# First expert's differences all on VectorE, its successor's chunks loaded under the projection, the first tile's splits dealt out later

## The chip, the cores and the metric

One Trainium2 chip, one of its cores. The metric is the time of one execution on the device in microseconds (us), the median of the runs; smaller is better. TensorE does the matmuls and transposes (PE; its weight loads are PEld), VectorE (DVE), ScalarE (ACT) and GpSimd (POOL) work elementwise, SyncE (SP) issues transfers. Each engine takes its instructions in program order, and so does each engine's queue of transfers it issues.

## The reference, cut to what matters

Attention with a mask of hash buckets gives x (1536 tokens of 512), a first layer takes the largest of three products, and a second layer sends each token to one of eight experts:

```
attn_out = _attn_ref(q, k, v, proj)                    # 2 x 8 heads x 768 x 64
x = attn_out.transpose(0, 2, 1, 3).reshape(1536, 512)
h = maximum(maximum(x @ w1, x @ w2), x @ w3)           # 1536 x 768
x = h @ w_out                                          # the projection, 1536 x 512
out = x
for tokens with x @ w_skip > 0:
    e = argmax(x @ w_gate)                             # one of 8 experts
    out += softmax weight of e * (relu(x @ w1[e]) @ w2[e])   # 512 -> 1024 -> 512
```

## The kernel before, in words

All matmuls of the two layers work on splits: a float32 value is cut into a high part of TensorE's fp32r type and the rest, and a product is made of three matmuls (high by high, high by low, low by high). A split is two instructions, a copy on ScalarE that makes the high part and a subtraction that makes the low part.

The stretch around the change has two stages. The first is the projection, the loop over T in `fused_kernel` (lines 264 to 291): twelve tiles of 128 tokens, 18 matmuls each (line 270) into one of four accumulators `po`. After them `gsplit` splits the input of tile T + 2 (ScalarE line 164, VectorE line 165), a step of the routing is issued (T = 0 to 5), ScalarE evacuates `po` into one of three buffers `x2` (line 278; the last tile on VectorE, line 280), and SyncE writes `x2` twice, to `x2d` for later gathers and to the output (lines 281 and 282). Then come one chunk load and, in tiles 2 to 9, two splits of expert 0's weights. The routing's fourth step (T = 3) has GpSimd scatter the tokens' places into a list, twelve indirect transfers (line 481), and load the list back as `LT` (line 488). After tile 8 GpSimd gathers the first 128 rows of expert 0 into `xf[0]` by that list, if they all lie in the first nine tiles (line 513).

The second stage is `moe2`: for each expert a tile of its first 128 tokens, then as many extra tiles as it needs. With these inputs the trace shows one tile for each expert, five extra ones for expert 0 and one for expert 7. A tile transposes its rows and splits them (`turn`, lines 546 and 550, 551), multiplies by w1 in two halves (`mm1`, line 570), takes the relu on ScalarE (line 575), transposes and splits the hidden rows (`hidden`), multiplies by w2 (`mm2`, line 583), weighs and adds (`finish`, line 588) and scatters the rows to the output (line 590). The rows of an expert's first extra tile, `xe`, are gathered by GpSimd (line 513 in `pull`) in the middle of its first tile.

Each expert's weights are eight chunks of 512 KB, chunk i of expert e being number 8 e + i. A chunk lies in a ring slot until it is split, by 16 splits k = 0 to 15 for an expert, two for a chunk (line 375 on ScalarE, line 377 on VectorE, or on GpSimd for k in `POOLK` = 3, 7, 11, 15). The second split of a chunk frees its slot. The ring has five slots under the projection and nine in `moe2`. `load` takes the next chunk if a slot is free and otherwise does nothing; its transfer waits on SyncE until the slot's last split is done. In an expert's first tile the next expert's 16 splits are dealt out at five places by `aside(k)`, k splits with a load behind each. The order of all instructions is the program's; nothing is rearranged.

Of the kernel before, what the change touches and what calls it, by code (L numbers as in the profile page):

```python
# [89 lines left out]
def fused_kernel(ctx, tc, qk, qz, v, vt, proj, cst, pat, w123, wo, woT, wg, e1, e2, out, upto=9, dbg=None):  # L90
# [68 lines left out]
    def gsplit(T):  # L159
        pool, bufs = (tpool, 2) if T % 3 else (gpool, 1)  # L160
        h = pool.tile([P, NF1, P], F32R, tag="gh", name="gh", bufs=bufs)
        l = pool.tile([P, NF1, P], F32R, tag="gl", name="gl", bufs=bufs)
        src = g[:, :, T * P:(T + 1) * P]
        nc.scalar.activation(out=h, in_=src, func=AF.Copy)
        nc.vector.tensor_tensor(out=l, in0=src, in1=h.bitcast(F32), op=ALU.subtract)
        gs[T] = h, l
# [3 lines left out]
    with tc.tile_pool(name="wpb", bufs=1, side=LEFT, reuse_waits="tile") as wpb:  # L170
# [32 lines left out]
        for f in range(NF1):  # L203
# [4 lines left out]
            for j in range(NBLK):  # L208
                b, a = divmod(j * BLK, S)
                pts = []  # L210
                for w in range(3):
                    pt = ps1.tile([P, BLK], F32, tag="m", name="m", bufs=6)
                    pts.append(pt)
                    n = 0
# [31 lines left out]
        for i in range(2):  # L246
            a, e = 512 * i, min(512 * i + 512, S)
# [7 lines left out]
    m2 = Moe2Weights(tc, nc, e1, e2, m2p)  # L255
# [4 lines left out]
    with tc.tile_pool(name="ps2", bufs=1, space=PSUM, reuse_waits="tile") as ps:  # L260
        steps = routing(tc, nc, ps, tpool, rpool, zs, wlg, g, ident, onesb, trib, cc, lst, rt)
        m2.load(3)
        gsplit(1)
        for T in range(NTT):
            po = ps.tile([P, DM], F32, tag="po", name="po", bufs=4)
            h, l = gs.pop(T)
            n = 0
            for f in range(NF1):
                for a, r in ((h, woh), (h, wol), (l, woh)):
                    nc.tensor.matmul(po, lhsT=a[:, f], rhs=r[f], start=(n == 0), stop=(n == 3 * NF1 - 1))  # L270
                    n += 1
            if T + 2 < NTT:
                gsplit(T + 2)
            if steps:
                steps.pop(0)()
            x2 = tpool.tile([P, DM], F32, tag="x2", name="x2", bufs=3)
            if T + 1 < NTT:
                nc.scalar.activation(out=x2, in_=po, func=AF.Copy)
            else:
                nc.vector.tensor_copy(out=x2, in_=po)  # L280
            nc.sync.dma_start(out=x2d[T * P:(T + 1) * P, :], in_=x2)
            nc.sync.dma_start(out=out[T * P:(T + 1) * P, :], in_=x2)
            m2.load(min(1, Moe2Weights.NCH - m2.loaded))
            for k in SPLITS.get(T, ()):
                m2.split(0, k)
            if T == EARLY:
                rt["plan"] = [nc.values_load(rt["plan"][0:1, e:e + 1], engines=ENGINES) for e in range(E2)]
            if T == EARLY - 1:
                early = nc.values_load(rt["early"], engines=[mybir.EngineType.Pool])
                with tc.If(early > 0):  # L290
                    fetch(nc, xf[0], x2d[0:EARLY * P], rt["LT"][:, 0])
# [23 lines left out]
class Moe1Weights:  # L315
# [20 lines left out]
    def split(self, f, w, pool, tag, bufs):  # L336
        self.narrow(f, w, pool, tag, bufs)
        self.halves(f, w)


class Moe2Weights:
# [29 lines left out]
    def split(self, e, k):  # L371
        i, q = divmod(k, 2)
        a = slice(q * 512, q * 512 + 512)
        h, l, r = self.hi[e % 2][i][:, a], self.lo[e % 2][i][:, a], self.raw[e, i][:, a]
        self.nc.scalar.activation(out=h, in_=r, func=AF.Copy)  # L375
        eng = self.nc.gpsimd if k in POOLK else self.nc.vector
        eng.tensor_tensor(out=l, in0=r, in1=h.bitcast(F32), op=ALU.subtract)  # L377
        if q:
            self.free.append(self.raw.pop((e, i)))
# [11 lines left out]
def routing(tc, nc, ps, pool, keep, zs, wlg, g, ident, onesb, trib, cc, lst, rt):  # L391
    def fold():
        t2 = ps.tile([P, NF1, 32], F32, tag="t2", name="t2", bufs=1)
        for f in range(NF1):
            nc.tensor.matmul(t2[:, f], lhsT=zs[:, f * P:(f + 1) * P], rhs=cc[:, 32:64],
                             start=True, stop=True, skip_group_check=True)
        nc.scalar.activation(out=wlg, in_=t2, func=AF.Copy)

    def logits():
        lg = ps.tile([P, BLK], F32, tag="lg", name="lg", bufs=1)  # L400
        for f in range(NF1):
            for j in range(NBLK):
                nc.tensor.matmul(lg[32 * j:32 * j + 32, :], lhsT=wlg[:, f], rhs=g[:, f, j * BLK:(j + 1) * BLK],
                                 start=(f == 0), stop=(f == NF1 - 1), skip_group_check=True)
        rt["lgs"] = pool.tile([P, BLK], F32, name="lgs")
        nc.scalar.activation(out=rt["lgs"], in_=lg, func=AF.Copy)

    return [fold, logits, *route(tc, nc, ps, pool, keep, rt, ident, onesb, trib, cc, lst)]
# [103 lines left out]
def fetch(nc, xg, x2d, m):  # L512
    nc.gpsimd.indirect_dma_start(out=xg, out_offset=None, in_=x2d,  # L513
                                 in_offset=bass.IndirectOffsetOnAxis(ap=m[:, 0:1], axis=0))


def moe2(tc, nc, m2, ident, rt, XF, x2d, out):
# [8 lines left out]
    with tc.tile_pool(name="ps3", bufs=1, space=PSUM, reuse_waits="tile") as ps:  # L526
# [7 lines left out]
        def enlist(e):  # L534
            nc.gpsimd.tensor_copy(out=PL[0][:, 0:CMAX - 1], in_=LT[:, e * CMAX + 1:(e + 1) * CMAX])  # L535
# [24 lines left out]
        def hidden(d, n):  # L560
            d["hT", n] = h, l = [pool.tile([P, 4, P], F32R, tag="t" + x, name="t" + x, bufs=2) for x in "hl"]
            halves(turn(d["r", n]), h, l)

        def mm1(d, n, cr):
            if ("h", n) not in d:
                d["h", n] = ps.tile([P, 512], F32, tag="h", name="h", bufs=3)
            h, l = d["x"]
            for c in cr:
                for i, (a, lo) in enumerate(((h, 0), (h, 1), (l, 0))):
                    nc.tensor.matmul(d["h", n], lhsT=a[:, c], rhs=m2.w1(d["e"], c, n, lo),  # L570
                                     start=(c == 0 and i == 0), stop=(c == NC1 - 1 and i == 2))

        def relu(d, n):
            d["r", n] = pool.tile([P, 512], F32, tag="r", name="r", bufs=2)
            nc.scalar.activation(out=d["r", n], in_=d["h", n], func=AF.Relu)

        def mm2(d, fr):
            if fr[0] == 0:
                d["y"] = ps.tile([P, DM], F32, tag="y", name="y", bufs=2)
            for f in fr:  # L580
                h, l = d["hT", f // 4]
                for i, (a, lo) in enumerate(((h, 0), (h, 1), (l, 0))):
                    nc.tensor.matmul(d["y"], lhsT=a[:, f % 4], rhs=m2.w2(d["e"], f, lo),  # L583
                                     start=(f == 0 and i == 0), stop=(f == NF2 - 1 and i == 2))

        def finish(d):
            ot = d["xg"]
            nc.vector.scalar_tensor_tensor(out=ot, in0=d["y"], scalar=d["m"][:, 2:3].bitcast(F32),
                                           in1=ot, op0=ALU.mult, op1=ALU.add)
            nc.gpsimd.indirect_dma_start(  # L590
                out=out, out_offset=bass.IndirectOffsetOnAxis(ap=d["m"][:, 1:2], axis=0),
                in_=ot, in_offset=None, bounds_check=NT - 1, oob_is_err=False)

        def tile(d, aside=lambda k: None, ahead=lambda: None, then=lambda: None):
            aside(4)
            mm1(d, 0, (0, 1, 2, 3))
            relu(d, 0)
            aside(4)
            mm1(d, 1, (0, 1))
            hidden(d, 0)  # L600
            mm1(d, 1, (2, 3))
            relu(d, 1)
            ahead()
            aside(4)
            mm2(d, (0, 1))
            hidden(d, 1)
            aside(3)
            mm2(d, (2, 3))
            then()
            aside(1)  # L610
            mm2(d, (4, 5, 6, 7))
            finish(d)

# [25 lines left out]
        for e in range(E2):  # L639
            todo = list(range(16)) if e + 1 < E2 else []  # L640

            def aside(k):
                for j in todo[:k]:
                    m2.split(e + 1, j)
                    m2.load(1)
                del todo[:k]

            m2.load(sum(RING) if e == 0 else 0)

            def ahead():  # L650
                enlist(e)
                pull(0)
                hint(e, 0)

            def then():
                prepare(e + 1)
                gather(e + 2)

            tile(tiles[e], aside, ahead, then)
            extras(tiles[e])  # L660
# [415 lines left out]
ENGINES = [mybir.EngineType.PE, mybir.EngineType.Activation, mybir.EngineType.DVE, mybir.EngineType.Pool]  # L1076
EARLY = 9
SPLITS = {T: (2 * T - 4, 2 * T - 3) for T in range(2, 10)}
POOLK = (3, 7, 11, 15)
def lay_out(q, k, v, proj, moe_w1, moe_w2, moe_w3, moe_w_out, moe2_w_skip, moe2_w_gate, moe2_w1, moe2_w2):  # L1080
    tr = [a.transpose(0, 1, 3, 2).reshape(B * NPAIR, 2, D, S) for a in (q, k)]
# [36 lines left out]
```

## Time and profile before

| | us |
|---|---|
| median of 3 runs | 713.81 |
| lowest and highest | 713.08 and 721.5 |
| the profiled execution, whole | 718.32 |
| its span, first to last instruction | 716.5 |
| busy in it: TensorE | 654.8 (91%) |
| VectorE | 421.4 (59%) |
| ScalarE | 336.9 (47%) |
| GpSimd | 317.1 (44%) |
| mean granted TensorE clock | 0.966 |

The profile is one execution; the rows below are from it, with times counted from the start of its span. Its own time lies between the lowest and the highest of the runs. The page cuts the span into 40 slices of 17.9 us; TensorE's busy tenths stand there beside the clock, the transfers and the other engines, and the views by instruction, by wait and by transfer tell what is behind a slice.

### The profile page before, as it was taken

Reading aid. Unit: us, or ns where it says so; the run is one execution under the profiler, and the core shown is the slowest. Engines: PE = TensorE matmul, PEld = TensorE weight load, DVE = VectorE, ACT = ScalarE, POOL = GpSimd, SP = SyncE. Lnnn points to the kernel's source line nnn. Section 1 sums busy time; section 2 is a strip of 40 time slices with the busy share of each in tenths; the row PEclk is TensorE's granted clock in tenths of the full one; section 3 lists DMA queues with packets and bytes.
Section 4 is the critical chain, followed back from the end, with each engine's and each line's share of the span. In section 5 each row is a group of like instructions: output and inputs, shape, how many; then the busy total and the mean of one; then the engine's idle time right before and its main releaser. Section 6 shows DMA issues by size and latency. Waiting matters only on the chain. (4 is left out here: it accounts for less than half of the span.)

```text
span 716.5 us, 9581 instructions
## 1 busy us (share of the span) xinstructions
PE 654.8 (91%) x3361; PEld 479.9 (67%) x3361; DVE 421.4 (59%) x648; ACT 336.9 (47%) x648; POOL 317.1 (44%) x250
## 2 busy tenths in 40 slices
PE   6789999999999988999999999987899988987784
PEld 2544555555555547999999997865688866665563
DVE  4696868878785582656656652723422267777611
ACT  6664666766665651323222312533422256766521
POOL 2494767767677760322221200452512055555630
PEclk9798999999999999999999999999999999999997
DMA  6444314213003003114303133348911047667510
GB/s 250 166 155 138 104 45 155 68 47 108 23 1 114 0 1 148 46 74 147 136 29 130 60 118 110 126 149 302 403 39 44 31 167 271 223 242 259 192 45 12
DMA packets 31472, 87.40 MB, mean 122 GB/s; under 512 B 4066, under 2 KB 4450, under 8 KB 30608
## 3 DMA queue, kind: packets, MB, share of 16 engines
q1 hardware_dynamic: 28144, 78.21, 30.9%
q0 software_dynamic: 3232, 8.07, 3.7%
q8 instruction: 40, 0.66, 0.4%
q14 instruction: 56, 0.46, 0.2%
HBM read 77.35 MB, written 10.18 MB: 122 GB/s over the span
## 5 line engine op out<-in xcount | busy, mean ns | idle before, releaser
L831 POOL TENSOR_TENSOR sum<-sum,Pt 128x768 f32<-128x768 f32 x60 | 116.8, 1950 | 33.6 <-ACT Pt L826 33.5
L826 ACT ACTIVATE Pt<-psb 128x384 f32<-128x384 f32 x192 | 83.8, 488 | 65.7 <-PE psb L824 64.8
L791 DVE TENSOR_REDUCE negm<-psa 128x1 f32<-128x768 f32 x86 | 82.0, 954 | 46.6 <-PE psa L789 46.3
L217 PE MATMUL m<-xh,whi 128*128 128x384 f32 x288 | 98.3, 341 | 3.0 <-DVEq L922 2.9
L377 DVE TENSOR_TENSOR w2l<-ring,w2h 128x512 fp32r<-128x512 f32 x96 | 76.0, 839 | 40.5 <-ACT w2h L375 36.6
L217 PE MATMUL m<-xl,whi 128*128 128x384 f32 x288 | 97.3, 338 | 0.0
L217 PE MATMUL m<-xh,wlo 128*128 128x384 f32 x288 | 97.3, 338 | 0.0
L375 ACT ACTIVATE w2h<-ring 128x512 fp32r<-128x512 f32 x128 | 72.0, 622 | 29.0 <-DMA ring<-in_dram 14.8
L838 PE MATMUL pso<-Pt,V 128*64 128x384 f32 x384 | 83.8, 518 | 0.2 <-DVE negm L791 0.2
L822 PE MATMUL psb<-S 128*128 128x384 f32 x192 | 76.5, 398 | 0.3 <-ACT S L766 0.3
L822 PEld LDWEIGHTS psb<-S 128*128 128x128 f32 x192 | 37.2, 194 | 54.1 <-ACT Pt L826 21.5
L824 PE MATMUL psb<-S 128*128 128x384 f32 x192 | 66.1, 344 | 0.0
L377 POOL TENSOR_TENSOR w2l<-ring,w2h 128x512 fp32r<-128x512 f32 x32 | 43.9, 1382 | 45.5 <-ACT w2h L375 14.3
L217 PEld LDWEIGHTS m<-xh,whi 128*128 128x128 f32 x288 | 54.6, 190 | 6.0 <-DVEq L922 3.5
L583 PE MATMUL y<-w2h,th 128*128 128x512 f32 x112 | 49.1, 439 | 6.5 <-ACT th L550 5.8
L217 PEld LDWEIGHTS m<-xl,whi 128*128 128x128 f32 x288 | 54.7, 190 | 0.0
L217 PEld LDWEIGHTS m<-xh,wlo 128*128 128x128 f32 x288 | 54.5, 189 | 0.0
L583 PE MATMUL y<-w2h,tl 128*128 128x512 f32 x112 | 47.1, 421 | 7.9 <-DVE tl L551 7.9
L334 POOL TENSOR_TENSOR wlo<-wide,whi 128x512 fp32r<-128x512 f32 x18 | 23.4, 1300 | 69.4 <-ACT whi L333 54.2
L551 DVE TENSOR_TENSOR tl<-tp,th 128x512 fp32r<-128x512 f32 x28 | 19.3, 688 | 56.4 <-ACT th L550 51.2
L570 PE MATMUL h<-w2h,xh 128*128 128x512 f32 x112 | 46.2, 413 | 5.5 <-ACTq L619 2.6
L789 PE MATMUL psa<-S 128*128 128x512 f32 (+1 forms) x172 | 47.6, 359 | 0.9 <-ACT S L766 0.8
(185 smaller groups left out, 1219.2 us busy)
## 6 DMA issues: line engine op xcount, KB each, us to landing
ring<-in_dram SPq DMA_DIRECT2D x64, 512.0 KB, 6.2
R<-in_dram SPq DMA_DIRECT2D x32, 384.0 KB, 3.1
wraw<-in_dram SPq DMA_DIRECT2D x6, 1536.0 KB, 6.4
Z<-in_dram SPq DMA_DIRECT2D x16, 384.0 KB, 5.5
V<-in_dram SPq DMA_DIRECT2D x8, 384.0 KB, 3.6
oraw<-in_dram SPq DMA_DIRECT2D x6, 512.0 KB, 3.4
traw<-in_dram SPq DMA_DIRECT2D x6, 512.0 KB, 4.3
x2d<-x SPq DMA_DIRECT2D x12, 256.0 KB, 2.3
```

The lines of the kernel that those rows point to most:

```text
L217: nc.tensor.matmul(pt, lhsT=l[:, w, c], rhs=r[b][c][:, a:a + BLK], start=(n == 0), stop=(n == 3 * NC1 - 1))
L375: self.nc.scalar.activation(out=h, in_=r, func=AF.Copy)
L377: eng.tensor_tensor(out=l, in0=r, in1=h.bitcast(F32), op=ALU.subtract)
L570: nc.tensor.matmul(d["h", n], lhsT=a[:, c], rhs=m2.w1(d["e"], c, n, lo), start=(c == 0 and i == 0), stop=(c == NC1 - 1 and i == 2))
L583: nc.tensor.matmul(d["y"], lhsT=a[:, f % 4], rhs=m2.w2(d["e"], f, lo), start=(f == 0 and i == 0), stop=(f == NF2 - 1 and i == 2))
L789: nc.tensor.matmul(tl[:, a:e], lhsT=S1[:, h, t * P:(t + 1) * P], rhs=S1[:, 2 + h, a:e], start=True, stop=True, skip_group_check=True)
L791: nc.vector.tensor_reduce(out=d["negm"][:, t, h:h + 1], in_=tl[:, 0:S], axis=AX.X, op=ALU.max, negate=True)
L822: nc.tensor.matmul(tl, lhsT=S1[:, 2 + h, k * P:(k + 1) * P], rhs=S1[:, h, cut(j)], start=True, stop=False, skip_group_check=True)
L824: nc.tensor.matmul(tl, lhsT=S2[:, 2 + h, k * P:(k + 1) * P], rhs=S2[:, h, cut(j)], start=False, stop=True, skip_group_check=True)
L826: nc.scalar.activation(out=pt[:, cut(j)], in_=tl, func=AF.Exp, scale=0.125)
L831: eng.tensor_tensor(out=d["sum", h], in0=d["P", h, 0] if k == 1 else d["sum", h], in1=pt, op=ALU.add)
L838: nc.tensor.matmul(d["o"][64 * h:64 * h + 64, i], lhsT=d["V"][:, k, h], rhs=d["P", h, k][:, i * BLK:(i + 1) * BLK], start=(k == 0), stop=( ...
```

## The change

Three edits. Under the projection `m2.load(1)` runs in every tile, so chunks of expert 1 follow those of expert 0 as slots come free. The subtractions of expert 0's splits are all VectorE's; for other experts k = 3, 7, 11 and 15 stay GpSimd's. And `aside` takes the number of the place instead of a count: in expert 0's first tile the counts are 0, 4, 4, 4, 4, in the others 4, 4, 4, 3, 1 as before.

```
-            m2.load(min(1, Moe2Weights.NCH - m2.loaded))
+            m2.load(1)
...
-        eng = self.nc.gpsimd if k in POOLK else self.nc.vector
+        eng = self.nc.gpsimd if e and k in POOLK else self.nc.vector
...
-        def tile(d, aside=lambda k: None, ahead=lambda: None, then=lambda: None):
-            aside(4)
+        def tile(d, aside=lambda n: None, ahead=lambda: None, then=lambda: None):
+            aside(0)
             mm1(d, 0, (0, 1, 2, 3))
             relu(d, 0)
-            aside(4)
+            aside(1)
             mm1(d, 1, (0, 1))
             hidden(d, 0)
             mm1(d, 1, (2, 3))
             relu(d, 1)
             ahead()
-            aside(4)
+            aside(2)
             mm2(d, (0, 1))
             hidden(d, 1)
             aside(3)
             mm2(d, (2, 3))
             then()
-            aside(1)
+            aside(4)
             mm2(d, (4, 5, 6, 7))
             finish(d)
...
-            def aside(k):
+            def aside(n):
+                k = DEAL[e > 0][n]
                 for j in todo[:k]:
                     m2.split(e + 1, j)
                     m2.load(1)
...
+DEAL = (0, 4, 4, 4, 4), (4, 4, 4, 3, 1)
```

## Rows read from the trace of the kernel before

**Rows 1.** Timeline, TensorE: start, us, line, operation, [idle before, what ended it].
```profile
483.80 0.79 PE L270 MATMUL po<-woh,gh 128*128 128x512 f32 x1 [2.85 <-ACT gh L164]
...
490.64 0.63 PE L546 MATMUL tp<-cs,xf 128*128 128x128 f32 x4 [0.92 <-DMA lst<-dt,posi]
491.95 0.50 PE L570 MATMUL h<-w2h,xh 128*128 128x512 f32 x1 [0.69 <-ACT xh L550]
...
503.51 0.50 PE L583 MATMUL y<-w2h,th 128*128 128x512 f32 x1 [2.55 <-ACT th L550]
...
512.58 0.63 PE L546 MATMUL tp<-cs,xe 128*128 128x128 f32 x4 [0.64 <-DMA xe<-x2d,pm]
513.89 0.50 PE L570 MATMUL h<-w2h,xh 128*128 128x512 f32 x1 [0.69 <-ACT xh L550]
```

**Rows 2.** Windows: busy us of PE, PEld, DVE, ACT, POOL, granted clock, DMA share, GB/s.
```profile
484.00:486.00 2.00, 2.00 (x5) 1.32 (x6) 1.43 (x2) 1.61 (x3) 0.00 (x0) 0.50 0.93 360
```

**Rows 3.** Timeline, ScalarE, projection and first expert tile.
```profile
464.72 0.60 ACT L278 ACTIVATE x<-po 128x512 f32<-128x512 f32 x1 [1.71 <-issue]
...
468.80 0.60 ACT L278 ACTIVATE x<-po 128x512 f32<-128x512 f32 x1 [1.71 <-issue]
...
481.38 0.60 ACT L278 ACTIVATE x<-po 128x512 f32<-128x512 f32 x1 [10.21 <-DMA out_dram<-x]
...
496.02 2.35 ACT L375 ACTIVATE w2h<-ring 128x512 fp32r<-128x512 f32 x4 [4.13 <-DMA ring<-in_dram]
```

**Rows 4.** Timeline, SyncE's queue, the load of chunk 6.
```profile
475.21 0.38 SPq L368 DMA_DIRECT2D ring<-in_dram  x1
```

**Rows 5.** Timeline, GpSimd, projection and first expert tile.
```profile
470.54 0.98 POOL L481 DMA_INDIRECT lst<-dt,posi  x1 [0.31 <-issue]
473.27 0.59 POOL L488 DMA_DIRECT2D LT<-lst  x1 [1.76 <-PE po L270]
473.88 3.78 POOL L377 TENSOR_TENSOR w2l<-ring,w2h 128x512 fp32r<-128x512 f32 x3
486.61 1.00 POOL L513 DMA_INDIRECT xf<-x2d,LT  x1 [8.95 <-DMA x2d<-x]
...
503.05 1.28 POOL L377 TENSOR_TENSOR w2l<-ring,w2h 128x512 fp32r<-128x512 f32 x1 [3.32 <-ACT w2h L375]
...
505.50 1.15 POOL L513 DMA_INDIRECT xe<-x2d,pm  x1 [0.27 <-POOL pm L538]
```

**Rows 6.** VectorE's splits, projection, then experts 2 on: ns least/median/most, first and last start.
```profile
L377 DVE TENSOR_TENSOR w2l<-ring,w2h x12: 629/692/695, 450.1 to 485.1; 128x512 fp32r<-128x512 f32 x12
...
L377 DVE TENSOR_TENSOR w2l<-ring,w2h x60: 676/691/2197, 595.9 to 674.9; 128x512 fp32r<-128x512 f32 x60
```

**Rows 7.** Timeline, ScalarE: four splits in a row, then the extra tile after.
```profile
503.83 2.19 ACT L375 ACTIVATE w2h<-ring 128x512 fp32r<-128x512 f32 x4
...
517.32 0.60 ACT L575 ACTIVATE r<-h 128x512 f32<-128x512 f32 x1 [3.48 <-PE h L570]
519.14 0.60 ACT L550 ACTIVATE th<-tp 128x512 fp32r<-128x512 f32 x1 [1.23 <-PE tp L546]
```

**Rows 8.** Timeline, VectorE: end of that extra tile; a later tile with splits.
```profile
526.95 0.75 DVE L588 SCALAR_TENSOR_TENSOR xe<-y,pm,xe 128x512 f32<-128x512 f32 x1 [1.45 <-PE y L583]
...
613.28 3.70 DVE L377 TENSOR_TENSOR w2l<-ring,w2h 128x512 fp32r<-128x512 f32 x6 [3.20 <-DVEq L619]
...
624.69 0.73 DVE L588 SCALAR_TENSOR_TENSOR xf<-y,LT,xf 128x512 f32<-128x512 f32 x1
```

**Rows 9.** Transfers, us from issue to landing: LT, the xe at 505.50, the xf at 493.36, all of xe.
```profile
LT<-lst POOLq DMA_DIRECT2D x1, 192.0 KB, 2.7
...
xe<-x2d,pm POOLq DMA_INDIRECT x1, 6.9
...
xf<-x2d,LT POOLq DMA_INDIRECT x1, 8.0
...
DMA to landing us min/median/max: 2.6/3.2/8.3
```

More of the change, by code (lines that the diff above doesn't have):

```diff
@@ L282, in fused_kernel @@
             nc.sync.dma_start(out=out[T * P:(T + 1) * P, :], in_=x2)
-            m2.load(min(1, Moe2Weights.NCH - m2.loaded))
+            m2.load(1)
             for k in SPLITS.get(T, ()):
@@ L375, in split @@
         self.nc.scalar.activation(out=h, in_=r, func=AF.Copy)
-        eng = self.nc.gpsimd if k in POOLK else self.nc.vector
+        eng = self.nc.gpsimd if e and k in POOLK else self.nc.vector
         eng.tensor_tensor(out=l, in0=r, in1=h.bitcast(F32), op=ALU.subtract)
@@ L592, in finish, with tile @@
                 in_=ot, in_offset=None, bounds_check=NT - 1, oob_is_err=False)
-        def tile(d, aside=lambda k: None, ahead=lambda: None, then=lambda: None):
-            aside(4)
+        def tile(d, aside=lambda n: None, ahead=lambda: None, then=lambda: None):
+            aside(0)
             mm1(d, 0, (0, 1, 2, 3))
             relu(d, 0)
-            aside(4)
+            aside(1)
             mm1(d, 1, (0, 1))
@@ L603, in tile @@
             ahead()
-            aside(4)
+            aside(2)
             mm2(d, (0, 1))
@@ L609, in tile @@
             then()
-            aside(1)
+            aside(4)
             mm2(d, (4, 5, 6, 7))
@@ L640, in moe2, with aside @@
             todo = list(range(16)) if e + 1 < E2 else []
-            def aside(k):
+            def aside(n):
+                k = DEAL[e > 0][n]
                 for j in todo[:k]:
@@ L1078 @@
 SPLITS = {T: (2 * T - 4, 2 * T - 3) for T in range(2, 10)}
+DEAL = (0, 4, 4, 4, 4), (4, 4, 4, 3, 1)
 POOLK = (3, 7, 11, 15)
```

## The prediction

> **What bounds the kernel now.** The span of 716.5 us and TensorE's 91% of it stand in the table of before. I read the page's slices first: TensorE is busy in nearly all of them except two near 480 to 515 us, which is where the output projection ends and expert 0's first tile runs. All three edits lie there, so the rest was read as one question: which wait ends last between 450 us and the start of expert 0's second tile.
>
> TensorE's timeline [rows 1] gives the losses. It stops at 480.95 (483.80 less the 2.85 idle) before the last projection tile, which starts at 483.80. That tile ends at 489.72 (490.64 less 0.92). Tile after tile comes 4.08 us apart in the evacuations of ScalarE [rows 3], so without the stop it would end at 485.03: 4.69 us are lost, 2.85 as idle time and 1.84 because the tile ran partly at half speed; the granted clock is 0.50 in 484 to 486, the 1.2 GHz level, right behind the idle [rows 2]. A further 0.92 us goes before the first transposes. Then, inside expert 0's first tile, TensorE waits for ScalarE (the larger stall is 2.55 us at 503.51), and for a gather at 512.58. Write M for the first matmul of a tile's mm1: 491.95 for the first tile, 513.89 for the next, 21.94 us apart [rows 1].
>
> Why it stops is read in three queues. ScalarE cannot evacuate tile 8 until 481.38: 10.21 us for a buffer of x2 whose write to out has not landed [rows 3]. That write stood in SyncE's queue behind a ring load that was issued only at 475.21 [rows 4]. That load wanted the slot of chunk 1, whose second half (k = 3) is GpSimd's; GpSimd's queue holds the twelve scatters of the routing list (the last at 470.54), then the load LT that waits for them (473.27), and only then three of these splits in one go, 473.88 to 477.66 [rows 5]. Twelve like them on VectorE took 629 to 695 ns meanwhile [rows 6]. In the first tile the cause is another: all of expert 1's chunks are asked for only behind the projection, and ScalarE, in order, stands 4.13 us at its first split for a chunk, with the relu behind it [rows 3].
>
> **The change, part by part.** *First expert's differences on VectorE.* Four GpSimd instructions of 1.26 us (3.78 for three [rows 5]) go, four of 0.63 to 0.70 [rows 6] come to VectorE, 2.8 us in all over four projection tiles of 4.08. VectorE has the room: two splits (2 x 0.69) and one difference of 768 columns where a split has 512 (some 1.0) make 2.4 us a tile. Cost nothing; were that cover gone, 0.7 us a tile. The slots come free in the tile that splits them, so SyncE no longer stands in front of x2d and out, ScalarE evacuates every 4.08 us, and the projection ends at 485.03. What is late next is the gather of the first tile's rows, below.
>
> *Loads under the projection.* Five loads of 512 KB (chunks 8 to 12) move from behind the projection to its tiles 6 to 10; tiles 2 and 11 find no free slot. Each is one instruction on SyncE, in front of the next tile's x2d and out. A tile then moves 256 + 256 + 512 KB in 4.08 us, 257 GB/s, against 360 in the stretch of [rows 2]; the out write has three tiles to land. Nothing on TensorE's path, then; but scatters, LT and the gather of xf share the engines. GpSimd, free of splits, issues that gather when LT and x2d of tile 8 have landed. LT goes at 473.27 as before; the last scatter is not moved. LT took 2.7 us to land [rows 9] and tile 8's x2d would be out near 476, so the gather goes at about 477 instead of 486.61 [rows 5]. Gathers land in 2.6 to 8.3 us [rows 9], so 480 to 485: ready. The first M is 485.03 + 1.31 (490.64 to 491.95) = 486.3, **5.65 us earlier**.
>
> *Splits dealt out late.* The first tile does none before mm1, then 4, 4, 4, 4; the ones that stay with GpSimd here are still k = 3, 7, 11, 15. Their chunks 8 to 12 lie in the ring, 13 to 15 are asked for at about M and used 10 us later, so no split waits for a transfer. In a tile without splits the relu starts at M + 3.43 and the halves of the first hidden transposes at M + 5.25 (517.32 and 519.14 [rows 7] against 513.89). Four splits (2.19 us) now lie between them: 3.43 + 0.6 + 2.19, so the halves start at about M + 6.2, 0.95 later, and mm2 as much. A tile without splits ends TensorE's work at about M + 12.9 (VectorE's finish at 526.95 [rows 8]), so this one at M + 13.8. The last four splits, put ahead of mm2's second half, delay ScalarE and VectorE only in front of the next tile's halves, which have another wait:
>
> *the gather xe.* The next tile's rows are fetched by GpSimd behind split k = 3. ScalarE ends that split's half at M + 6.2, GpSimd's takes 1.3, and from its end to the fetch it took 1.17 (503.05 + 1.28 to 505.50 [rows 5]), so the fetch goes at M + 8.7 to 9.0. The same fetch landed 6.9 us later [rows 9], when transfers filled the engines; splits free slots and start loads again here, so I take 6.9, not the 3.2 of a quiet stretch. Transposes at M + 15.9, next M at M + 17.2. TensorE thus idles some 2 us, where it now idles 0.64 at 512.58. Beside it VectorE begins its 12 splits only at M + 4.7; the tile in which it did such a set without a break took from 613.28 to 625.42 [rows 8], 12.1 us, which gives M + 16.8 and another 0.7 for the next xl: the same moment within 0.5. So next M = 486.3 + 17.2 = 503.5 against 513.89: **10.4 us earlier**. A wait of 2 us may again bring the half clock; that cost 1.84 once, and I put 0.4 on it. From there on the work is what it was: the ring ends with the same nine chunks of expert 2, and expert 0 has five extra tiles in which no split runs, so all later times move by the same **10 us**.
>
> A row and a rule part here. VectorE's splits took at most 695 ns while GpSimd only made descriptors, and up to 2197 once both split at the same time [rows 6]. The Trainium skill (SBUF — State Buffer, "Who interferes with whom") says that a VectorE instruction with two SBUF inputs and a GpSimd instruction that reads SBUF exclude each other for a whole instruction. The two maxima agree with that, the medians do not show it. By it the dense dealing of the first tile is a disadvantage, with the result under rival B.
>
> **The rivals.** *A: the list is late.* The five loads share the engines with the scatters, LT and xf. At the far ends: LT 1.6 us later, landing and x2d at about 480, the gather at its 8.0 [rows 9], so rows at 488, not 485. For it: x2d and out now see loads all the time; against it: 257 of 360 GB/s. It costs 3 us: gain 7, 706.8 us.
>
> *B: VectorE's splits are held by GpSimd's.* Four GpSimd splits, each holding up one of VectorE's by 0.7 to 1.5 us (2197 less 690 [rows 6]), add 3 to 6 to a queue of 12 splits (8.3 us) and four others (2.8) that begins at M + 4.7, against 1 to 2 in the set above. End at about M + 20, the next M some 3 us later: gain 7, 706.8. Against it: the set from 613.28 had the same instructions.
>
> *C: no wait is left.* The gather lands in 3.2 to 4 us and TensorE runs the tile through: next M = 486.3 + 13.8 + 1.31 = 501.4, gain 12.5; without the 0.95 too, 13.4: 700.4.
>
> *D, on the other side: slower.* The dealing moves VectorE's 12 splits behind M + 4.7. If each took the 2.2 us of the slowest [rows 6], the queue would end at M + 4.7 + 26.4 + 2.8 = M + 33.9 and the next tile at 520.2, 6.3 us later than now: 720. It decides only from a mean of 1.7 us a split on (503.5 + 10.4 is 513.9; 20.1 us for 12), and the median of sixty of them, taken beside GpSimd's, is 0.69 [rows 6].
>
> *E: the stop stays.* If SyncE still meets a slot that is not free (a load per tile, each behind the splits of the tile before), the projection keeps its 4.69 us; the gain is only the first tile's 4.8: 709. Against it: by the sums above VectorE has each tile's splits done within the tile.
>
> **How the numbers follow.** The profiled execution took 718.32 us, 1.8 more than its span; 718.3 - 10 = 708.3 is its successor. The median shown is 713.81, 0.6% below; nothing in the profile ties this difference to the stretch, so the same 10 us come off: **703.8 us**, 1.4% less. A difference of about 2% is what a measurement of this kernel can tell from no change; that would be 699.5, a gain of 14.3, beyond C. Chances: forecast (gain 8.5 to 12.5, 701.3 to 705.3) 0.60, A 0.13, B 0.12, C 0.07, D 0.03, E 0.05. The range takes in C at its best (700.4) and E (709), with a little for the spread of the runs (713.08 to 721.5): 699.5 to 710. Faster by over 2% needs C and a favourable median: 0.12; slower by over 2%, D and an unfavourable one: 0.03; within 2%: 0.85.
>
> **What would show it.** Right: no GpSimd split before 495 us; SyncE's loads of chunks 6 to 12 at intervals of about 4.1 us from 458; evacuation of tile 8 at about 473; last projection tile ending near 485 at clock 1.00; ScalarE's first split for expert 1 behind the first relu without a wait for a transfer; a wait for xe of about 2 us before the second tile, whose M is near 503.5; from there each row about 10.4 us earlier. A shows as idle time before the first transposes; B as VectorE splits well over 1 us and a wait for xl or tl; C as no wait for xe; E as x2d issues in a bunch. The prediction is wrong if the projection's stop had a second cause under the one found, if the gather of xe lands far from 6.9, or if a clock drop follows its wait.

## The result and the profile after

The changed kernel took 708.78 us (median of 4 runs, 703.32 to 711.92) beside 714.52 for the kernel before in the same comparison: a ratio of 0.987, with a 95% interval of 0.983 to 0.992, a gain of 5.5 to 12.5 us. That is faster, by less than 2%, and inside the range; the forecast was 703.8, and the narrow band around it (701.3 to 705.3, given 0.60) was missed. A second comparison (experiment 5) gave 0.991 (0.988 to 0.994). The quotient of the two medians above is 0.992, at the weak end of the first interval. Of the traces below, experiment 1's alone is of a slow run (721.76 us), so it is read beside experiment 10's.

Two stretches that the change does not touch move by themselves from trace to trace. The projection's first matmul, called P from here on, lies at 429.25 us before and at 425.24 in the profile after (423.4 to 431.3 in the experiments), and the last eight tiles (VectorE's finish of expert 0's last extra tile to its last finish of all) take 128 to 135 us in kernels that differ nowhere there. So 4.0 of the 12.1 us between the two spans (716.5 and 704.4) come from ahead of the change and 1.2 from far behind it. The change is therefore read from P to VectorE's finish of the second tile, expert 0's first extra one, called F: 97.70 us before (526.95 less 429.25 [rows 8]), 90.94 after (516.18 less 425.24). **Its own gain is 6.8 us, where the prediction had 10.**

TensorE's timeline of the kernel after, to be read against [rows 1]:

```profile
481.86 0.63 PE L546 MATMUL tp<-cs,xf 128*128 128x128 f32 x4 [0.84 <-DMA lst<-dt,posi]
483.18 0.50 PE L570 MATMUL h<-w2h,xh 128*128 128x512 f32 x1 [0.69 <-ACT xh L550]
...
498.34 0.63 PE L546 MATMUL tp<-cs,xe 128*128 128x128 f32 x4 [1.65 <-DMA xe<-x2d,pm]
499.65 0.50 PE L570 MATMUL h<-w2h,xh 128*128 128x512 f32 x1 [0.69 <-ACT xh L550]
502.31 0.78 PE L570 MATMUL h<-w2h,xl 128*128 128x512 f32 x1 [1.92 <-DVE xl L551]
```

The stop ahead of the last projection tile is gone: no row with idle time stands between P and 481.86. The first tile's M is 57.94 behind P (62.70 before), the tile takes 16.47 us (21.94), and neither of its old waits for ScalarE's relu and hidden rows is left. Then comes a row that the kernel before did not have: the second tile has hardly begun when it waits 1.92 us for xl, the low part of its rows. What follows shows in the windows (columns as in [rows 2]):

```profile
500.00:502.00 2.00, 0.39 (x2) 0.00 (x0) 2.00 (x4) 0.00 (x0) 0.06 (x1) 1.00 1.00 333
502.00:504.00 2.00, 1.69 (x4) 1.40 (x5) 0.26 (x1) 0.00 (x0) 1.73 (x3) 0.59 1.06 396
504.00:506.00 2.00, 2.00 (x6) 1.55 (x6) 0.00 (x0) 0.00 (x0) 0.89 (x3) 0.56 0.97 385
```

The granted clock falls to 0.59 and 0.56, most of it at the 1.2 GHz level, where the stretch before it was at 1.00. From its own M to F the second tile takes 16.53 us instead of 13.06: 1.92 of wait and, as the rest, 1.55 of half clock. Its M had come 10.2 us early (P + 74.41, before P + 84.64), so 6.8 is left.

The queues ahead of it did what was worked out. ScalarE's evacuation of tile 8 and SyncE's queue, against [rows 3, 4]:

```profile
468.93 0.60 ACT L278 ACTIVATE x<-po 128x512 f32<-128x512 f32 x1 [0.63 <-ACT gh L164]
...
486.53 0.60 ACT L575 ACTIVATE r<-h 128x512 f32<-128x512 f32 x1 [3.41 <-PE h L570]
487.02 2.19 ACT L375 ACTIVATE w2h<-ring 128x512 fp32r<-128x512 f32 x4
```

```profile
454.06 0.41 SPq L368 DMA_DIRECT2D ring<-in_dram  x1
...
458.14 0.41 SPq L368 DMA_DIRECT2D ring<-in_dram  x1
...
462.22 0.72 SPq L365 DMA_DIRECT2D ring<-in_dram  x1
```

Tile 8 of the projection is evacuated at 468.93, that is P + 43.7 against P + 52.1 (481.38). The load of chunk 6 goes at 454.06 (P + 28.8, before P + 46.0) and the next ones one to a tile. The first split for expert 1 stands right behind the first relu and waits for nothing.

VectorE and GpSimd in the first tile of the kernel after:

```profile
487.68 1.90 DVE L377 TENSOR_TENSOR w2l<-ring,w2h 128x512 fp32r<-128x512 f32 x3 [3.83 <-ACT w2h L375]
...
493.56 4.12 DVE L377 TENSOR_TENSOR w2l<-ring,w2h 128x512 fp32r<-128x512 f32 x3
497.60 0.68 DVE L551 TENSOR_TENSOR xl<-tp,xh 128x512 fp32r<-128x512 f32 x1
498.20 2.79 DVE L377 TENSOR_TENSOR w2l<-ring,w2h 128x512 fp32r<-128x512 f32 x3
500.92 0.74 DVE L588 SCALAR_TENSOR_TENSOR xf<-y,LT,xf 128x512 f32<-128x512 f32 x1
501.58 0.68 DVE L551 TENSOR_TENSOR xl<-tp,xh 128x512 fp32r<-128x512 f32 x1
```

```profile
489.30 1.42 POOL L377 TENSOR_TENSOR w2l<-ring,w2h 128x512 fp32r<-128x512 f32 x1 [2.69 <-ACT w2h L375]
...
491.92 1.15 POOL L513 DMA_INDIRECT xe<-x2d,pm  x1 [0.27 <-POOL pm L538]
...
493.54 1.29 POOL L377 TENSOR_TENSOR w2l<-ring,w2h 128x512 fp32r<-128x512 f32 x1
495.08 1.46 POOL L377 TENSOR_TENSOR w2l<-ring,w2h 128x512 fp32r<-128x512 f32 x1 [0.25 <-ACT w2h L375]
...
497.96 1.27 POOL L377 TENSOR_TENSOR w2l<-ring,w2h 128x512 fp32r<-128x512 f32 x1
```

Three splits of VectorE take 1.90 us with GpSimd's beside them for 0.3 us at most, and 4.12 from 493.56 on, when two of GpSimd's run in the same time; three more take 2.79 beside the next. VectorE has no idle time between 492.95 and 502.26, and the xl of the second tile is its last instruction there. This is rival B.

### The profile page after: what moved, and what is told of

It is laid out like the page before. It is cut to its first block, busy times and chain, and to the rows that moved or that the text cites. A ratio compares the mean times of both kernels' runs of the same rounds, so it can differ in the third digit from the quotient of the medians.

```text
span 704.4 us, 9584 instructions
## 1 busy us (share of the span) xinstructions
PE 649.9 (92%) x3361; PEld 476.7 (68%) x3361; DVE 421.7 (60%) x652; ACT 336.3 (48%) x648; POOL 311.4 (44%) x246
## 5 line engine op out<-in xcount | busy, mean ns | idle before, releaser
L375 ACT ACTIVATE w2h<-ring 128x512 fp32r<-128x512 f32 x128 | 71.7, 623 | 20.9 <-PEq L619 11.3
L377 POOL TENSOR_TENSOR w2l<-ring,w2h 128x512 fp32r<-128x512 f32 x28 | 38.8, 1393 | 40.6 <-DMA ring<-in_dram 20.5
L570 PE MATMUL h<-w2h,xh 128*128 128x512 f32 x112 | 48.1, 429 | 6.0 <-ACTq L619 2.7
L583 PE MATMUL y<-w2h,tl 128*128 128x512 f32 x112 | 45.6, 407 | 4.4 <-DVE tl L551 4.3
L570 PE MATMUL h<-w2h,xl 128*128 128x512 f32 x112 | 46.1, 412 | 1.9 <-DVE xl L551 1.9
```

## The experiments

The numbers are from one trace each, in us behind P, beside the ratio to the kernel before where a kernel was timed. "Tile" is M to the next M.

| kernel | M | tile | F | ratio (95%) |
|---|---|---|---|---|
| before | 62.70 | 21.94 | 97.70 | |
| after | 57.94 | 16.47 | 90.94 | 0.987 (0.983 to 0.992) |
| 1 differences only | 57.14 | 23.00 | 95.09 | 0.996 (0.991 to 1.001) |
| 10 the same again | 57.19 | 22.26 | 94.05 | |
| 2 loads only | 65.81 | 18.72 | 98.80 | 1.002 (0.997 to 1.007) |
| 3 after, dealt early | 56.91 | 17.67 | 88.84 | 0.990 (0.985 to 0.994) |
| 4 after, expert 1 on VectorE | 56.91 | 15.17 | 88.35 | 0.989 (0.984 to 0.994) |
| 5 after again | 56.91 | 16.55 | 90.78 | 0.991 (0.988 to 0.994) |
| 6 after without the loads | 57.15 | 19.92 | 91.87 | |
| 7 after, xe gathered first | 56.91 | 14.92 | 90.27 | |
| 8 early and expert 1 on VectorE | 56.91 | 15.06 | 85.04 | 0.986 (0.980 to 0.992) |
| 9 no GpSimd split at all | 56.91 | 15.71 | 85.68 | 0.975 (0.970 to 0.980) |

The ratios of 3, 4, 5 and 8 cannot be told apart: differences of 2 to 6 us are about the width of their intervals. What tells them apart is F.

**1 and 10. VectorE's differences alone.**

```
-        eng = self.nc.gpsimd if k in POOLK else self.nc.vector
+        eng = self.nc.gpsimd if e and k in POOLK else self.nc.vector
```

> The kernel before with one part of the change: expert 0's differences all on VectorE; loads and dealing as before. Times are counted from P, the first matmul of the projection (before: first expert tile's M at P + 62.7, next tile's M at P + 84.6, VectorE's finish of the second tile at P + 97.7; after: 57.9, 74.4, 90.9). My theory, that the projection stopped only because ring slots 1, 3, 5, 7 waited for GpSimd: no stop, M at P + 57 to 58, the first tile as long as before (21.9 us, its chunks still asked for late), finish at P + 93, about 4.7 us (0.7%) faster than before. Rival, that the projection's transfers or x2 buffers would stop it anyway, or that the early loads are needed: M stays at P + 62 or later and the time does not move.

M came at P + 57.1: the stop had only the cause that was found, GpSimd's splits behind the scatters. The tile stayed long, and F was at 95.1, not 93.

> The kernel before with expert 0's differences on VectorE alone, once more. Its first trace had M at P + 57.1, a first tile of 23.0 us and the second tile's finish at P + 95.1, where 93 had been expected. If the tile's stalls (3.15 us for the first relu, 2.4 for xe, half clock behind both) belong to the kernel: 94.5 to 95.5 again. If they are chance: 93.

94.05, between the two. Its TensorE timeline:

```profile
489.44 0.66 PE L546 MATMUL tp<-cs,r 128*128 128x128 f32 x4 [2.72 <-ACT r L575]
493.72 0.50 PE L583 MATMUL y<-w2h,th 128*128 128x512 f32 x1 [2.23 <-ACT th L550]
```

The old stalls of the tile are all there (2.72 and 2.23 us behind ScalarE, which waits 4.56 us for its first chunk, with the first relu behind it). Of the 5.5 us gained at M, 1.9 to 3.0 are given back by F, through a first tile that is 0.3 to 1.1 us longer and a second one that is 1.5 to 1.9 longer, part of it at half clock (0.50 in 506 to 508 of this trace).

**2. The loads alone.**

```
-            m2.load(min(1, Moe2Weights.NCH - m2.loaded))
+            m2.load(1)
```

> The kernel before with only the loads under the projection; GpSimd keeps its four splits of expert 0 and the dealing is as before. Same clock P. My theory: the stop stays and may grow by the loads that now stand in SyncE's queue behind GpSimd's slots, M at P + 62.5 to 65; the first tile no longer waits for its first chunks, 16 to 17 us instead of 21.9, so next M at P + 79 to 81 and finish at P + 92 to 95, some 4 us faster than before. Rival, that the loads alone undo the stop: M at P + 58. Rival, that the first tile was not held by its chunks: it stays at 21.9 us and the finish is at P + 97 or later.

The stop stayed, as expected, and something was added that had not been: M is 3.1 us later than before.

```profile
481.18 0.79 PE L270 MATMUL po<-woh,gh 128*128 128x512 f32 x1 [2.32 <-ACT gh L164]
...
491.16 1.12 PE L546 MATMUL tp<-cs,xf 128*128 128x128 f32 x4 [4.10 <-DMA xf<-x2d,LT]
```

The gather of the first tile's rows is issued only at 487.00 and TensorE waits 4.10 us for it, with the half clock behind. The loads that waited for GpSimd's slots all go between 473 and 484, together with the held-up x2d writes on which that gather depends; that it is late by these loads is the likely reading, not shown apart. The first tile gets shorter by 3.2 us (18.72, not the 16 to 17 expected, since its first relu ends 2.0 us later behind M than in the changed kernel, at half clock), and the two cancel at the next M. The second tile is 1.2 us longer than before, with half clock behind a wait of 1.93 us for xe: F at 98.80, ratio 1.002. The expected gain of 4 us was wrong, for the most part by that gather and the half clock behind it.

**3. The first tile's splits dealt as in the others.**

```
-DEAL = (0, 4, 4, 4, 4), (4, 4, 4, 3, 1)
+DEAL = (4, 4, 4, 3, 1), (4, 4, 4, 3, 1)
```

> The changed kernel with the first tile's splits dealt out as in the other tiles (4, 4, 4, 3, 1). Same clock P. My theory, that VectorE's queue in the first tile ended too late because its splits begin only behind the first relu: VectorE starts 4.7 us sooner, the wait of the second tile for xl (1.92 us) and the half clock behind it vanish, finish of the second tile at P + 87 to 88 instead of 90.9, some 3.5 us faster than the changed kernel. Rival, that late dealing protects the first relu or TensorE's transposes: the first tile gets stalls of its own and the finish is at P + 91 or later.

The wait for xl vanished, but F came at 88.84, not at 87 to 88, because GpSimd's queue, with the gather xe in it, took the place of VectorE's:

```profile
502.71 0.63 PE L546 MATMUL tp<-cs,xe 128*128 128x128 f32 x4 [2.81 <-DMA xe<-x2d,pm]
```

**4. Expert 1's differences on VectorE too** (the dealing stays late).

```
-        eng = self.nc.gpsimd if e and k in POOLK else self.nc.vector
+        eng = self.nc.gpsimd if e > 1 and k in POOLK else self.nc.vector
```

> The changed kernel with expert 1's differences (done in the first expert tile) all on VectorE as well, so GpSimd does no split there. Same clock P. Lock theory (a GpSimd split holds a VectorE split that runs beside it): no VectorE split of the tile over 0.75 us although VectorE has four more, the gather xe is issued 1.3 us sooner, wait for xl under 0.7 us, second tile's finish at P + 86.5 to 88. Rival (the queue is simply long): four more splits of 0.69 make it longer by 2.8 us, the wait for xl grows to about 4 us and the finish is at P + 93 or later.

VectorE's rows in the first tile:

```profile
498.94 2.49 DVE L377 TENSOR_TENSOR w2l<-ring,w2h 128x512 fp32r<-128x512 f32 x4
501.34 0.68 DVE L551 TENSOR_TENSOR xl<-tp,xh 128x512 fp32r<-128x512 f32 x1
501.94 2.48 DVE L377 TENSOR_TENSOR w2l<-ring,w2h 128x512 fp32r<-128x512 f32 x4
504.35 0.74 DVE L588 SCALAR_TENSOR_TENSOR xf<-y,LT,xf 128x512 f32<-128x512 f32 x1
505.01 0.68 DVE L551 TENSOR_TENSOR xl<-tp,xh 128x512 fp32r<-128x512 f32 x1
```

Four splits take 2.5 us where three had taken 4.12: 0.62 each. None of the sixteen takes over 0.71 us. So GpSimd's splits do hold VectorE's. With four more splits its queue ends 1.6 us sooner behind M (505.69 less 488.18, 17.5, against 502.26 less 483.18, 19.1). The gather xe, issued 4.76 behind M instead of 8.74, makes the tile 1.3 us shorter. But the wait for xl is still 1.66 us, more than the lock theory allowed (0.7), and far less than the rival's 4: a queue that begins 4.5 us behind M is too long even without the lock. F is at 88.35, just behind the 88 of the lock theory.

**5. The change once more.**

> The changed kernel as it is, once more, to see what of its trace repeats. P is the first matmul of the projection. If the 0.84 us in front of its first transposes and the 1.92 us for xl belong to the kernel: M at P + 57.9, finish of the second tile at P + 90.9, within 0.3. If the gather xf lands as chance has it: no wait in front of the transposes, M at P + 56.9, the rest as before with M, so the finish at P + 90. If the wait for xl is chance too: P + 87.

The wait for xl repeats (1.85 us, F at 90.78); the 0.84 us in front of the first transposes does not (M at 56.91, as in every other trace with all of the first two edits). That part of rival A was chance.

**6. The change without the loads.**

> The changed kernel without the loads under the projection: nine chunks are asked for at M, as in the kernel before. My theory, that the loads are what the first tile gains by: dealing late moves the first split from M to M + 4.5 where its chunk has just landed, but the nine loads and the gathers then share the engines; splits wait for chunks by 1 to 3 us or the gather xe lands late, finish at P + 92 to 94 (90.9 with the loads, 95.1 with VectorE's differences alone). Rival, that late dealing alone is enough and the loads are idle: finish at P + 90 to 91.5.

F at 91.87: 1.0 us behind the change, between the two expectations. ScalarE waits twice for a chunk, 1.1 us each, and neither of the two holds the first relu:

```profile
490.24 2.36 ACT L375 ACTIVATE w2h<-ring 128x512 fp32r<-128x512 f32 x4 [1.09 <-DMA ring<-in_dram]
...
495.74 1.15 ACT L375 ACTIVATE w2h<-ring 128x512 fp32r<-128x512 f32 x2 [1.13 <-DMA ring<-in_dram]
```

TensorE still loses 1.39 us for the hidden rows behind the first of them and 2.63 us for xe, so the next M comes only at P + 77.07; by then VectorE's queue has caught up, and no wait for xl follows.

With VectorE's differences in place, six traces make a square (F):

| | no early loads | early loads |
|---|---|---|
| dealt early (4, 4, 4, 3, 1) | 95.1, 94.1 | 88.8 |
| dealt late (0, 4, 4, 4, 4) | 91.9 | 90.9, 90.8 |

The loads and the late dealing are two cures for one stall, ScalarE's wait for a chunk with the first relu behind it: TensorE waits 2.72 and 3.15 us for that relu in the two traces with neither, and not at all in the others. Alone, the loads bring 5 to 6 us and the late dealing 2 to 3. On top of the loads the late dealing costs 2, since then it only puts off VectorE's queue.

**7. The gather xe issued first**, ahead of all splits of the first tile.

```
         prepare(0)
         gather(1)
+        enlist(0)
+        pull(0)
...
-                enlist(e)
-                pull(0)
+                if e:
+                    enlist(e)
+                    pull(0)
```

> The changed kernel with the gather xe of expert 0 issued at the front of its first tile, behind the gather of expert 1's rows and ahead of all splits, instead of behind split k = 3. My theory, that VectorE's queue sets when the second tile can use xl: the wait for xe (1.65 us) vanishes, the wait for xl grows by as much, finish at P + 90 to 91, no gain. Rival, that the gather is what the second tile is late by: M of the second tile at P + 72.8 and finish at P + 88.5 to 89.3.

The next M came 1.6 us sooner than in experiment 5 (tile 14.92), the wait for xl grew by 1.1, and F was at 90.27, only 0.5 sooner:

```profile
504.17 0.80 PE L570 MATMUL h<-w2h,xl 128*128 128x512 f32 x1 [2.95 <-DVE xl L551]
```

VectorE's queue, not the gather, sets the end of the second tile in the changed kernel.

**8. Experiments 3 and 4 together.**

> The changed kernel with both: the first tile's splits dealt out 4, 4, 4, 3, 1 and expert 1's differences all on VectorE. My theory, that two queues set the second tile's start, GpSimd's (gather xe behind its splits) and VectorE's (xl behind its splits): both end early, no wait for either over 0.3 us, no half clock, the first tile 15 us and the second 13.1 from M to finish, finish at P + 85 to 86, some 5 us faster than the changed kernel. Rival, that one of the two waits comes back in another place (16 splits on VectorE, beginning at M): finish at P + 88 as with either alone.

F at 85.04, 5.7 to 5.9 us sooner than the change, with 13.07 us from the second tile's M to F: the row of that M is the last with idle time before F. The whole time does not show this gain: 0.986 beside 0.987 and 0.991 for the change.

```profile
498.42 0.50 PE L570 MATMUL h<-w2h,xh 128*128 128x512 f32 x1 [0.69 <-ACT xh L550]
```

**9. GpSimd does no split of any expert**, on top of experiment 8.

```
-POOLK = (3, 7, 11, 15)
+POOLK = ()
```

> The kernel with early dealing and expert 1 on VectorE, and the differences of all other experts on VectorE too: GpSimd does no split at all. The first tile stays as it is, finish of the second tile at P + 85. The eight later first tiles, from VectorE's finish of expert 0's last extra tile to its finish of the last tile of all, took 128 to 134.6 us in the traces so far, with VectorE splits up to 2.2 us. Lock theory: no split over 0.75 us, those tiles shorter by 0.5 to 1 us each where no chunk is late, 124 to 129 us. Rival, that chunks and gathers set those tiles, or that four more splits of 0.62 cost VectorE what the lock cost it: 128 to 134 as before.

The last eight tiles took 120.0 us (558.67 to 678.68, VectorE's finishes) beside 130.5 in experiment 8 and 128 to 135 in all the other traces, below the 124 to 129 expected, and the kernel 695.52 us, ratio 0.975. All of VectorE's splits in these tiles, and below them TensorE's three longest waits there in experiment 8 and its two longest in experiment 9 (us in total, times, longest):

```profile
L377 DVE TENSOR_TENSOR w2l<-ring,w2h x96: 673/686/707, 559.8 to 651.5; 128x512 fp32r<-128x512 f32 x96
```

```profile
PE y L583 <- DVE tl L551: 8.0, 5, 2.0
PE tp L546 <- DMA xe<-x2d,pm: 3.1, 1, 3.1
PE h L570 <- ACTq L619: 3.0, 2, 2.5
```

```profile
PE h L570 <- ACTq L619: 7.8, 3, 2.9
PE y L583 <- DVE tl L551: 2.2, 6, 0.4
```

No split is over 0.71 us, and TensorE's waits for tl fall from 8.0 to 2.2 us. The other waits partly offset each other: those for the gathers xe and xf (3.1 and 0.8 us) and for th (1.6) are gone, those behind ScalarE at line 619, the test for an extra tile, grow by 4.8. All waits together fall from 17.6 to 11.3 us, 6.3 of the 10.5; TensorE's busy time in these tiles falls by another 4.0 (111.6 to 107.6) for as many matmuls, at a mean granted clock of 0.97 instead of 0.93. Which of this the lock caused directly, and which came with it, was not taken apart. This version beats both kernels: its interval (0.970 to 0.980) lies below those of the change.

## Why the prediction was right, and where its sum was off

- **What bounds and why it stops**: right. Differences alone remove the stop (1, 10), loads alone don't (2). The projection ends at P + 55.79 (481.03); worked out were 485.03 less 429.25, 55.78.
- **First M**: 5.65 us gained were forecast; 4.76 in the first trace, 5.5 to 5.8 in the others.
- **Loads cost TensorE nothing**: right with the slots free, as here (M at 56.91 with them, 57.14 to 57.19 without); wrong without free slots (experiment 2, 3.1 us at M).
- **Gather xe**: issue at M + 8.74 (8.7 to 9.0 worked out), wait of 1.65 us (2), the next M 10.2 us early (10.4). Right. The "no GpSimd split before 495" of the list was careless; the first came at M + 6.1, as the sum itself had it.
- **The step that was mis-sized is VectorE's queue in the first tile.** Its start was right: M + 4.5, worked out M + 4.7. Its length was taken from the set at 613.28 [rows 8], 12.1 us, which with 0.7 for xl gave M + 17.5 and "the same moment within 0.5". It ended at M + 19.1, 1.9 us behind the need. In that set of before only three of the twelve splits ran beside splits of GpSimd (at 619.99, 3.01 us for two), and the other nine took 5.58 us:

```profile
613.28 3.70 DVE L377 TENSOR_TENSOR w2l<-ring,w2h 128x512 fp32r<-128x512 f32 x6 [3.20 <-DVEq L619]
...
617.50 1.88 DVE L377 TENSOR_TENSOR w2l<-ring,w2h 128x512 fp32r<-128x512 f32 x3
...
620.59 3.58 DVE L377 TENSOR_TENSOR w2l<-ring,w2h 128x512 fp32r<-128x512 f32 x3
```

  In the changed kernel six did, and the twelve took 10.7 us instead of 9.2. The same instructions were no measure, because they had met GpSimd's at other moments.
- **Rival B**, given 0.12, had this mechanism and its place. Its price, "gain 7" beside 6.8 measured, is partly luck: B had the next M 3 us late, but that M was on time, and 1.92 us of wait and 1.55 of half clock came behind it.
- **The half clock** was entered with 0.4 for the wait for xe. Behind that wait the clock stayed at 1.00; the 1.55 came with the wait for xl, which the sum did not have.
- **C, D, E** did not happen. A showed in one trace out of the seven that have the first two edits, with 0.84 us instead of 3.
- That the time lies in the range is no proof of the sum: the range reached from C at its best to E. The profiled execution (706.31 us) came nearer to the 708.3 worked out for it than the change's own gain did, but 4 us of its difference come from ahead of P, in which this change has no part.

## What to carry to other kernels

Before moving work off a stretch, ask what it was covering there. Two edits that cure the same stall don't add up, and the second may cost (late dealing: 2 to 3 us gained without the loads, 2 lost with them). A queue on an engine off the critical path has a due time; add it up from the moment its first input exists, with the slow durations it will have beside its neighbours, not from a set that ran under other neighbours. And a slot that one engine frees late holds everything behind the load that wants it: here four splits of 1.3 us on GpSimd cost TensorE 4.7 us.

## What the runs showed of the hardware

A split of 128x512 on VectorE, both inputs in SBUF, takes 0.62 us in a row of four and up to 2.2 us beside a GpSimd split; three of them took 4.12 us beside two of 1.29 and 1.46. While GpSimd only issued scatters the longest was 0.70 [rows 6]. The Trainium skill (SBUF — State Buffer, "Who interferes with whom") says that a VectorE instruction with two SBUF inputs contends with a GpSimd instruction that reads SBUF, by an exclusive lock on the ports they share. The first tile of experiment 4 and all of experiment 9, in which no VectorE split is over 0.71 us once GpSimd does none, agree with it. What had not been expected is the sum: with 4 of 16 splits handed to the second engine the last eight tiles were 10.5 us longer (8 to 14.6 over all traces), and nothing was saved.

With the wait of TensorE of 1.92 us the granted clock fell to 0.56 to 0.59 for some 4 us, which cost 1.55 us; behind the 1.65 us ahead of it, it stayed at 1.00. The length of one wait does not decide this: in the kernel before, the clock was 1.00 behind 2.23 us (498.91) and 0.50 behind 2.55 us (503.51).
